# Writing the Fourier stage of the next group into the inverse's own tile, and keeping the inverse's matrices in SBUF

## The chip, the cores and the metric

One core of a Trainium2 chip runs the whole program. It has TensorE (PE, the products), VectorE (DVE), ScalarE (ACT), GpSimd (POOL) and SyncE (SP), which here only issues DMAs. The metric is the time of the device for one execution, in microseconds; runs of the kernel before lie between 3988.0 and 3996.9 us.

## The reference

Three parts in a row, all in float32. The change touches the first.

```
X = np.fft.rfft(x, axis=1)                     # x: 8 x 3072 x 256
Y = X * (filt_r + 1j * filt_i)[None]
y = np.fft.irfft(Y, n=3072, axis=1)            # then rows of 24576 tokens x 256
# routing: one of 8 experts by argmax of x @ w_gate, its gates, h = relu(x @ w1[e]) @ w2[e]
# then relu(x @ w_in)**2 @ w_out
```

## The kernel before

**Groups.** The 8 sequences go in four groups of two; the real and the imaginary part of a transform carry one sequence each. A sequence of 3072 is 64 x 48 (N1 x N2), so a transform is a first stage over 64 points with twiddles (48 products with a 128 x 128 matrix from `c_ma`), and a second stage over 48.

**Stage a** (`steps_a`, 12 steps a group, four of the 48 products each): x comes by DMA (`load_x`, 512 KB a step, two steps ahead). In group 0 the x tile is the stationary operand, so the product comes out with channels on the partitions; it is copied into `big`, an SBUF tile of 128 channels x 2 halves x 96 rows x 64 points (L269 to L274). In groups 1 to 3 the matrix is the stationary operand (L282); the product is copied into `ao` and written to rows in DRAM (`s1`, L287).

**Stage b** (`steps_b`, 32 units and a lag of three, so 35 steps a group), the middle stage. It takes two of the 64 points at a time. In group 0 `turn_b` transposes them out of `big` on PE (four transposes, L320) and copies them into `bi`, by turns on ScalarE and VectorE (L322). In groups 1 to 3 `load_b` reads `bi` from `s1` by DMA, four units ahead. Then `b_first` multiplies with the second stage's matrix (L347, L351), ScalarE copies the result crosswise into `q` (L353, L354), VectorE and GpSimd multiply with the filter (L355, L356); `b_mid` adds (L364), which frees the PSUM tile (three of them); `b_second` goes back through the inverse's first stage (L373) and ScalarE copies into `big` (L375), at the place of the two points. Each step issues the first part of one unit, the middle of the unit before and the second part of the unit three before.

**Stage c** (`steps_c`, 24 units and a lag of one, 25 steps a group), the inverse's last stage. A unit is two of the 48 rows. `c_turn` turns a row out of `big` and multiplies it with the gate weights (L394); `c_first` multiplies with the inverse's matrix (L410), a 512 KB tile for 8 rows. Those come by DMA, six a group and two buffers (`load_m(mi, ...)`, L403 and L538). After every four units `route` computes the gates and places of 8 x 128 tokens on VectorE with two small products on PE (L452, L462); the rows go to DRAM in one write of 1088 KB (L485), and 8 scatters of GpSimd (`scatter`, L423, two in each step of stage c) put the row numbers into one of four tables in DRAM by turns.

**The order.** All engines get their work in the order of one string, `order` (L526 to L547), a letter a step; each engine works through its own in that order. Group 0's 12 a steps stand first. Then, for each group, its 35 b steps and its 25 c steps; six a steps of the next group stand between the b steps (after 8, 16, 24 and the last three), six between the first c steps, and the first three b steps of the next group stand between the last three c steps. `ahead` holds loads to be issued at a place of the order. SP's queue takes the DMAs in the order of issue; a DMA that waits holds up those behind it. The experts' matrices and first products begin in the last group's stage c.

Of the kernel before, what the change touches and what calls it, by code (L numbers as in the profile page):

```python
# [23 lines left out]
E, F1 = 8, 1024  # L24
# [4 lines left out]
GC = D  # L29
PK = GC + 16  # L30
SEG = NT
# [69 lines left out]
def spectral_moe_kernel(ctx: ExitStack, tc: tile.TileContext, x, filt_r, filt_i, w_gate, w_og, w1, w2,  # L101
# [5 lines left out]
    dram = ctx.enter_context(tc.tile_pool(name="dram", bufs=1, space=DRAM))  # L107
    s1 = [dram.tile([96 * N1, PK], F32, name=f"s1_{g}") for g in range(NG)]
    yd = dram.tile([NT + 1, YW], F32, name="yd")
# [21 lines left out]
    cum_bf = const.tile([TC * E, TC * E + E], BF16, name="cum_bf")  # L131
    cum_f = const.tile([TC * E, TC * E + E], F32, name="cum_f")
    nc.scalar.dma_start(out=cum_f, in_=c_cum)
    nc.vector.tensor_copy(cum_bf, cum_f)

# [6 lines left out]
    for i in range(2):  # L142
# [21 lines left out]
    zrow = fcon.tile([1, YW], F32, name="zrow")  # L164
    nc.gpsimd.memset(zrow, 0.0)
    mb = fcon.tile([96, 2, 128], F32, name="mb")
    mb2 = fcon.tile([128, 2, 96], F32, name="mb2")
    sg = fcon.tile([128, 3], F32, name="sg")
    KF = 2
    NFB = 4  # L170
    fbuf = [fcon.tile([128, 2, KF, D], F32, name=f"fb{i}") for i in range(NFB)]
    map_, xp, aop, bip, qp = (right(fft, n, b) for n, b in (("map", 6), ("xp", 3), ("aop", 3), ("bip", 6), ("qp", 4)))
    psP = right(fft, "psP", 3, space=PSUM)
# [12 lines left out]
    mip, vtp, yop, rp, psA, psL = (inv.enter_context(tc.tile_pool(name=n, bufs=b, **kw)) for n, b, kw in (  # L186
        ("mip", 2, {}), ("vtp", 4, {}), ("yop", 4, {}), ("rp", 2, {}), ("psA", 3, {"space": PSUM}), ("psL", 1, {"space": PSUM})))
    big = ccon.tile([128, 2, 2 * N2, N1], F32, name="big")
# [65 lines left out]


    def steps_a():
        for u in range(len(aunits)):
            g, i = aunits[u]
            if g == 0 and i % 2 == 0 and i // 2 + 1 < 6:
                load_m(ma, c_ma, map_, i // 2 + 1)  # L260
            if u + 2 < len(aunits):
                load_x(u + 2)
            t = xt.pop(u)
            if g == 0:
                for h in range(JA // 2):
                    ps = psA.tile([128, 2, D], F32, name="p")
                    for j in range(2):
                        n = JA * i + 2 * h + j
                        for c in range(2):  # L269
                            at = (2 * h + j) * D + c * 128  # L270
                            nc.tensor.matmul(ps[:, c, j * 128:(j + 1) * 128], t[:, at:at + 128], ma[n // 8][:, n % 8, :])
                    n = 2 * (JA * i + 2 * h)
                    (nc.scalar.copy if h == 0 else nc.vector.tensor_copy)(
                        big[:, :, n:n + 4, :].rearrange("p c r k -> p c (r k)"), ps)  # L274
                yield
                continue
            ao = aop.tile([128, JA, D], F32, name="ao")
            for h in range(JA // 2):
                ps = psA.tile([128, 2, D], F32, name="p")
                for j in range(2):  # L280
                    n = JA * i + 2 * h + j
                    nc.tensor.matmul(ps[:, j], ma[n // 8][:, n % 8, :], t[:, (2 * h + j) * D:(2 * h + j + 1) * D])  # L282
                if h == 0:
                    nc.scalar.copy(ao[:, 0:2], ps)
                else:
                    nc.vector.tensor_copy(ao[:, 2:4], ps)
            later.append(lambda g=g, i=i, ao=ao: nc.sync.dma_start(  # L287
                out=s1[g][i * JA * 128:(i + 1) * JA * 128, 0:GC].rearrange("(j q) c -> q j c", j=JA), in_=ao))
            yield


    LAG = 3
    AB = 4
    s1v = [s.rearrange("(m k) c -> m k c", k=N1) for s in s1]
    ks = []
# [12 lines left out]

    def load_b(u):
        g, at = units[u][0], place(u)  # L310
        bi[u] = bip.tile([96, 2, D], F32, name="bi")
        nc.sync.dma_start(out=bi[u], in_=s1v[g][:, at:at + 2, 0:D])

    def turn_b(u):
# [9 lines left out]
    def b_first(u):  # L324
        g, ka, kb, w, up = units[u]
        v = u % UB
        if v + AB < UB and g:
            load_b(u + AB)
        if v == 0 or not up or v == UB - 1:
            nw = g * NW + w + 2  # L330
            for _ in fl[0]:
                pass
            if nw < NG * NW:
                fl[0] = load_f(nw)
        next(fl[0], None)
        next(fl[0], None)
        if v == UB - 1:
            for _ in fl[0]:
                pass
        if v == 0:  # L340
            dup_f(g * NW)
        if v == 0 or up and v < UB - 1:
            dup_f(g * NW + w + 1)
        f = fbuf[(g * NW + w) % NFB]
        p = psP.tile([128, 512], F32, name="p")
        if not up:
            nc.tensor.matmul(p, mb[:, up], bi.pop(u).rearrange("p k d -> p (k d)"))  # L347
        else:
            b = bi.pop(u)
            for k in range(2):  # L350
                nc.tensor.matmul(p[:, k * D:(k + 1) * D], mb[:, up], b[:, 1 - k])  # L351
        q = qp.tile([128, 512], F32, name="q")
        nc.scalar.copy(q[64:128], p[0:64])  # L353
        nc.scalar.copy(q[0:64], p[64:128])  # L354
        nc.vector.tensor_tensor(p, p, f[:, 0].rearrange("p k d -> p (k d)"), ALU.mult)  # L355
        nc.gpsimd.tensor_tensor(q, q, f[:, 1].rearrange("p k d -> p (k d)"), ALU.mult)  # L356
        pq[u] = p, q
# [42 lines left out]
    def c_first(u):  # L400
        g, j = cunits[u]
        if j % 4 == 0 and j + 4 < UC:
            load_m(mi, c_mi, mip, 6 * g + j // 4 + 1)  # L403
        c, s = divmod(u, 4)
        if s == 0:
            yo[c] = yop.tile([128, TC, YW], F32, name="yo")
        for i in range(2):
            n = 2 * j + i
            ps = (psL if i or g == NG - 1 else psO).tile([128, 512], F32, name="o")[:, 0:YW]
            nc.tensor.matmul(ps, mi[6 * g + n // 8][:, n % 8, :], vt.pop((u, i)))  # L410
            (nc.vector.tensor_copy if i else nc.scalar.copy)(yo[c][:, 2 * s + i], ps)
# [16 lines left out]
    def route(c):  # L428
# [3 lines left out]
        l = yo[c][:, :, HD:HD + 2 * E]  # L432
        m = rp.tile([128, TC, 1], F32, name="m")
        nc.vector.tensor_reduce(m[:, :, 0], l[:, :, 0:E], AX.X, ALU.max)
        d = rp.tile([128, TC, E], F32, name="d")
        nc.vector.tensor_tensor(d, l[:, :, 0:E], m.to_broadcast([128, TC, E]), ALU.subtract)
        cd = rp.tile([128, TC, E], F32, name="cd")
        nc.vector.scalar_tensor_tensor(cd, d, 0.0, rev, op0=ALU.is_ge, op1=ALU.mult)
        mx = rp.tile([128, TC, 1], F32, name="mx")
        nc.vector.tensor_reduce(mx[:, :, 0], cd, AX.X, ALU.max)  # L440
# [3 lines left out]
        nc.vector.tensor_copy(ob, oh.rearrange("p a e -> p (a e)"))  # L444
        z = rp.tile([128, TC, E], F32, name="z")
        nc.vector.tensor_tensor(z, oh, l[:, :, E:2 * E], ALU.mult)
# [20 lines left out]
        t = yo.pop(c)  # L467
        s = rp.tile([128, TC], F32, name="s")
        rk = rp.tile([128, TC, E], F32, name="rk")
        si = rp.tile([128, TC], I32, name="si", bufs=4)  # L470
        sl = rp.tile([128, TC], F32, name="sl")
        nc.vector.tensor_reduce(s, ex, AX.X, ALU.add)
# [17 lines left out]
    def steps_b():  # L490
        for g in range(NG):
            for u in range(g * UB, (g + 1) * UB + LAG):
                if u == 0:
                    turn_b(0)
                    turn_b(1)
                if u + 2 < UB:
                    turn_b(u + 2)
                if u < (g + 1) * UB:
# [26 lines left out]

    order = "a" * (UA + 0)  # L526
    ahead = {}
    for g in range(NG):
        next_a = lambda: "a" if g + 1 < NG and order.count("a") < (g + 2) * UA else ""
        nb = order.count("b") - g * (UB + LAG)  # L530
        first = len(order) - 2 if g == 0 else first_b
        if g:
            ahead.setdefault(first - (1 if g == 0 else 6), []).extend(lambda u=g * UB + i: load_b(u) for i in range(AB))
        for i in range(nb, UB + LAG):
            order += "b"
            if i in (8, 16, 24) or i >= UB:
                order += next_a()
        ahead.setdefault(len(order) - 8, []).append(lambda g=g: load_m(mi, c_mi, mip, 6 * g))  # L538
        for i in range(UC + LAGC):
            order += "c"  # L540
            if i in (1, 3, 6, 8, 11, 13):
                order += next_a()
            if i >= UC - 2 and g + 1 < NG:
                if i == UC - 2:
                    first_b = len(order)
                order += "b"
    order += "--"  # L547
# [617 lines left out]
```

## Time and profile before

| | |
|---|---|
| median of three runs | 3988.5 us (3988.0 to 3996.9) |
| profiled execution | 3993.0 us, its span 3991.3 us |
| PE busy, share of the span | 96% |
| VectorE, ScalarE, GpSimd | 70%, 50%, 20% |
| mean granted clock of PE | 0.979 |
| DMA, mean over the span | 92 GB/s |

The span is the time from the first to the last instruction in the trace. The shares are means over a transform part of some 730 us and two expert parts with other limits. A granted clock of 1.0 is 2.4 GHz, 0.5 is 1.2 GHz.

### The profile page before, as it was taken

To read this page: it belongs to the slowest core of one execution; us is meant where nothing else is said; L and a number is where in the kernel's file an instruction comes from. 1 tells how busy PE (TensorE), PEld (TensorE's weight loads), DVE (VectorE), ACT (ScalarE), POOL (GpSimd) and SP (SyncE) were. 2 spreads that over 40 slices of the span, in tenths; PEclk is the share of its full clock that TensorE was granted. 3 is DMA by queue.
4 is the path that set the end of the run, shared out by engine and by line. 5 is a ranking of instruction groups with operands and counts; after the bars stand their busy time and mean duration, and the time that the engine had idled before them with its cause. 6 is when DMAs were issued, how large, how long until landed. Compare 5 with 4: busy or idle time off the path is not lost.

```text
span 3991.3 us, 73834 instructions
## 1 busy us (share of the span) xinstructions
PE 3815.1 (96%) x26884; PEld 3538.1 (89%) x26884; DVE 2800.1 (70%) x5143; ACT 1979.2 (50%) x3909; POOL 778.6 (20%) x743
## 2 busy tenths in 40 slices
PE   8897977899999999999899999999999999999998
PEld 7775756688888888888899999999999999999998
DVE  6565665478888876666577777777777777777775
ACT  5453543245545455555455555555555555555554
POOL 3354555321111121111010100100101101001001
PEclk9988988999999999999999999999999999999999
DMA  6878864255556555555100000000000000000000
GB/s 198 206 182 185 205 147 117 53 165 164 166 163 174 168 168 161 158 164 158 56 26 27 26 29 22 28 28 22 28 28 24 26 28 26 29 22 27 28 17 17
DMA packets 311184, 365.86 MB, mean 92 GB/s; under 512 B 83329, under 2 KB 253538, under 8 KB 307746
## 3 DMA queue, kind: packets, MB, share of 16 engines
q1 hardware_dynamic: 284544, 306.91, 28.3%
q0 software_dynamic: 25248, 53.99, 4.5%
q8 instruction: 211, 3.46, 0.4%
q14 instruction: 155, 1.27, 0.1%
q10 hardware_dynamic: 1026, 0.23, 0.0%
HBM read 259.87 MB, written 101.13 MB: 90 GB/s over the span
## 4 chain that ended last, share of the span: by engine, by line
PE 81%; DMA 5%; DVE 3%; issue 2%; ACT 2%; POOL 1%; SPq 0%; another core or an unknown queue 0%; POOLq 0%; DVEq 0%; ACTq 0%
PE py L952 27%; PE ph L906 17%; PE ph L823 13%; PE py L839 13%; PE px L906 7%; DMA tab<-rowid,si 3%; PE o L410 1%; PE px L801 1%; PE p L351 1%; DVE q L364 1%; PE p L394 1%; DMA m<-c_mi_dram 1%; DVE p L355 1%; PE o L373 1%; PE p L282 0%
## 5 line engine op out<-in xcount | busy, mean ns | idle before, releaser
L952 PE MATMUL py<-woh,hh 128*128 128x256 f32 x3072 | 859.6, 280 | 0.0
L952 PE MATMUL py<-woh,hl 128*128 128x256 f32 x3072 | 857.0, 279 | 0.4 <-DVE hl L939 0.4
L952 PE MATMUL py<-wol,hh 128*128 128x256 f32 x3072 | 853.7, 278 | 0.0
L952 PEld LDWEIGHTS py<-woh,hh 128*128 128x128 f32 x3072 | 578.1, 188 | 0.0
L952 PEld LDWEIGHTS py<-wol,hh 128*128 128x128 f32 x3072 | 577.8, 188 | 0.0
L952 PEld LDWEIGHTS py<-woh,hl 128*128 128x128 f32 x3072 | 576.3, 188 | 0.9 <-DVE hl L939 0.8
L961 POOL DMA_INDIRECT out_dram<-ou,io x192 | 207.9, 1083 | 1886.5 <-ACT C L928 1651.3
L827 ACT ACTIVATE hh<-ph 128x512 fp32r<-128x512 f32 (+1 forms) x496 | 261.0, 526 | 612.4 <-PE ph L823 537.0
L906 PE MATMUL ph<-bh,wsh 128*128 128x256 f32 x1920 | 540.7, 282 | 9.8 <-ACT bh L883 5.7
L906 PE MATMUL ph<-bl,wsh 128*128 128x256 f32 x1920 | 538.6, 281 | 0.0
L906 PE MATMUL ph<-bh,wsl 128*128 128x256 f32 x1920 | 536.6, 279 | 0.0
L828 DVE SCALAR_TENSOR_TENSOR hl<-ph,hh 128x512 fp32r<-128x512 f32 (+1 forms) x496 | 296.7, 599 | 259.3 <-ACT hh L827 225.5
L930 DVE SCALAR_TENSOR_TENSOR q<-C 128x1024 f32<-128x1024 f32 x384 | 468.8, 1221 | 1.2 <-ACT C L928 1.2
L939 DVE TENSOR_TENSOR hl<-q,hh 128x1024 fp32r<-128x1024 f32 x384 | 467.0, 1216 | 1.1 <-ACT hh L937 1.1
L924 DVE TENSOR_TENSOR C<-ph,p 128x256 f32<-128x256 f32 x384 | 163.2, 425 | 412.4 <-ACT hh L937 331.9
L937 ACT CAST hh<-q 128x1024 fp32r<-128x1024 f32 x384 | 404.4, 1053 | 1.3 <-DVE q L930 1.3
L928 ACT COPY C<-ph 128x256 f32<-128x256 f32 x384 | 143.3, 373 | 503.6 <-PE ph L906 503.6
L763 POOL DMA_INDIRECT xg<-yd,idx x190 | 201.0, 1058 | 924.5 <-DVE idx L773 864.6
L906 PEld LDWEIGHTS ph<-bh,wsh 128*128 128x128 f32 x1920 | 360.6, 188 | 12.5 <-ACT bh L883 5.8
L906 PEld LDWEIGHTS ph<-bl,wsh 128*128 128x128 f32 x1920 | 362.1, 189 | 0.1
L839 PE MATMUL py<-hh,wh 128*128 128x512 f32 (+1 forms) x992 | 361.7, 365 | 0.0
L906 PEld LDWEIGHTS ph<-bh,wsl 128*128 128x128 f32 x1920 | 361.5, 188 | 0.0
(266 smaller groups left out, 8587.1 us busy)
## 6 DMA issues: line engine op xcount, KB each, us to landing
r<-in_moe_w_dram SPq DMA_DIRECT2D x472, 256.0 KB
yd<-yo SPq DMA_DIRECT2D x24, 1088.0 KB
xt<-in_x_dram SPq DMA_DIRECT2D x48, 512.0 KB
r<-ytd SPq DMA_DIRECT2D x48, 512.0 KB
ytd<-yt SPq DMA_DIRECT2D x41, 512.0 KB
s<-ao SPq DMA_DIRECT2D x36, 512.0 KB
bi<-s SPq DMA_DIRECT2D x96, 192.0 KB
m<-c_mi_dram SPq DMA_DIRECT2D x24, 512.0 KB
```

What stands on the lines that cost most here:

```text
L763: nc.gpsimd.indirect_dma_start(out=xg[:, c * YW:(c + 1) * YW], out_offset=None, in_=yd[0:(NT * GP // NG if t < KP else NT) + 1], in_offset ...
L823: nc.tensor.matmul(ps, a[:, c, f2 * 128:(f2 + 1) * 128], b[:, c, 0:w], start=n == 0, stop=n == 5)
L827: nc.scalar.activation(hh, ps, AF.Relu)
L828: nc.vector.scalar_tensor_tensor(hl, ps, 0.0, hh.bitcast(F32), op0=ALU.max, op1=ALU.subtract)
L839: nc.tensor.matmul(Y[t][h], a[:, f % 2, h * 128:(h + 1) * 128], b, start=f == 0 and i == 0, stop=f == NF - 1 and i == 2)
L906: nc.tensor.matmul(ps, x[:, u, a], y[:, b], start=start and n == 0, stop=n == 2, skip_group_check=True)
L924: nc.vector.tensor_tensor(C[:, 3], V, p5, ALU.add)
L930: nc.vector.scalar_tensor_tensor(q, C, 0.0, C, op0=ALU.max, op1=ALU.mult)
L937: nc.scalar.copy(hh, q)
L939: nc.vector.tensor_tensor(hl, q, hh.bitcast(F32), ALU.subtract)
L952: nc.tensor.matmul(Z[t][k][:, c, :], x[:, 2 * i + k, c * 128:(c + 1) * 128], w[:, 2 * u + i, :], start=u == 0 and m in (0, 6), stop=u == N ...
L961: nc.gpsimd.indirect_dma_start(out=out, out_offset=bass.IndirectOffsetOnAxis(ap=io[:, c:c + 1], axis=0), in_=ou[:, c, :], in_offset=None)
```

## The change

All four groups now have group 0's form of stages a and b: the product of stage a is copied into `big`, and stage b transposes out of it. `s1`, `ao`, `load_b` and their DMAs are gone. Since `big` still holds what stage c of the group before reads, the a steps of the next group all stand in stage c, one after every second c step: a step i writes the eight rows that c steps 2i and 2i+1 have turned. No a steps stand between b steps any more, and no b steps in stage c. Five of the 12 x tiles of the next group are loaded during stage b, the others five steps ahead (six x buffers in place of three). The inverse's six matrix tiles are loaded once, during group 0's stage b, and stay (six buffers in place of two). To make room, `bi` has four buffers in place of six, `vt` three in place of four, some scratch tiles of `route` one in place of two, and the tile `cum_f` is given back with the transform's others.

```diff
-    s1 = [dram.tile([96 * N1, PK], F32, name=f"s1_{g}") for g in range(NG)]
...
+    XB = 6
...
-    map_, xp, aop, bip, qp = (right(fft, n, b) for n, b in (("map", 6), ("xp", 3), ("aop", 3), ("bip", 6), ("qp", 4)))
+    map_, xp, bip, qp = (right(fft, n, b) for n, b in (("map", 6), ("xp", XB), ("bip", 4), ("qp", 4)))
...
-        ("mip", 2, {}), ("vtp", 4, {}), ("yop", 4, {}), ("rp", 2, {}), ("psA", 3, {"space": PSUM}), ("psL", 1, {"space": PSUM})))
+        ("mip", 6, {}), ("vtp", 3, {}), ("yop", 4, {}), ("rp", 2, {}), ("psA", 3, {"space": PSUM}), ("psL", 1, {"space": PSUM})))
...
+    XA = 2, XB - 1
+
     def steps_a():
         for u in range(len(aunits)):
             g, i = aunits[u]
             if g == 0 and i % 2 == 0 and i // 2 + 1 < 6:
                 load_m(ma, c_ma, map_, i // 2 + 1)
-            if u + 2 < len(aunits):
-                load_x(u + 2)
+            if i + XA[g > 0] < UA:
+                load_x(u + XA[g > 0])
             t = xt.pop(u)
...
-            ao = aop.tile([128, JA, D], F32, name="ao")
             for h in range(JA // 2):
                 ps = psA.tile([128, 2, D], F32, name="p")
                 for j in range(2):
                     n = JA * i + 2 * h + j
-                    nc.tensor.matmul(ps[:, j], ma[n // 8][:, n % 8, :], t[:, (2 * h + j) * D:(2 * h + j + 1) * D])
...
+                    for c in range(2):
+                        at = (2 * h + j) * D + c * 128
+                        nc.tensor.matmul(ps[:, c, j * 128:(j + 1) * 128], t[:, at:at + 128], ma[n // 8][:, n % 8, :])
+                n = 2 * (JA * i + 2 * h)
+                (nc.scalar.copy if h == 0 else nc.vector.tensor_copy)(
+                    big[:, :, n:n + 4, :].rearrange("p c r k -> p c (r k)"), ps)
             yield
...
-        if v + AB < UB and g:
-            load_b(u + AB)
...
-        if j % 4 == 0 and j + 4 < UC:
-            load_m(mi, c_mi, mip, 6 * g + j // 4 + 1)
...
-            nc.tensor.matmul(ps, mi[6 * g + n // 8][:, n % 8, :], vt.pop((u, i)))
+            nc.tensor.matmul(ps, mi[n // 8][:, n % 8, :], vt.pop((u, i)))
...
-                if u == 0:
-                    turn_b(0)
-                    turn_b(1)
-                if u + 2 < UB:
-                    turn_b(u + 2)
+                v = u - g * UB
+                for k in (0, 1, 2) if v == 0 else (v + 2,) if v + 2 < UB else ():
+                    turn_b(g * UB + k)
...
-        for i in range(nb, UB + LAG):
+        for i in range(UB + LAG):
+            if g == 0 and i >= 8 and i % 4 == 0 and i // 4 < 8:
+                ahead.setdefault(len(order), []).append(lambda i=i: load_m(mi, c_mi, mip, i // 4 - 2))
+            if g + 1 < NG and i % 5 == 3 and i // 5 < XB - 1:
+                ahead.setdefault(len(order), []).append(lambda u=(g + 1) * UA + i // 5: load_x(u))
             order += "b"
-            if i in (8, 16, 24) or i >= UB:
-                order += next_a()
-        ahead.setdefault(len(order) - 8, []).append(lambda g=g: load_m(mi, c_mi, mip, 6 * g))
         for i in range(UC + LAGC):
             order += "c"
-            if i in (1, 3, 6, 8, 11, 13):
-                order += next_a()
-            if i >= UC - 2 and g + 1 < NG:
-                if i == UC - 2:
-                    first_b = len(order)
-                order += "b"
+            if g + 1 < NG and i % 2 and i < UC:
+                order += "a"
     order += "--"
```

## Rows read from the trace of the kernel before

**Rows 1.** The page: busy us and share of the span by engine, instructions.
```profile
PE 3815.1 (96%) x26884; PEld 3538.1 (89%) x26884; DVE 2800.1 (70%) x5143; ACT 1979.2 (50%) x3909; POOL 778.6 (20%) x743
```

**Rows 2.** By stage: us, busy us by engine, granted clock, DMA share, GB/s.
```profile
0.00:38.47 38.47, 25.84 (x193) 24.52 (x193) 12.51 (x21) 8.31 (x13) 3.42 (x25) 1.00 0.88 284
38.47:120.68 82.21, 80.87 (x528) 69.78 (x529) 68.95 (x103) 64.75 (x118) 41.03 (x32) 1.00 0.48 146
120.68:195.56 74.88, 64.78 (x356) 54.55 (x355) 40.64 (x143) 26.51 (x73) 24.41 (x26) 0.93 0.87 226
195.56:283.00 87.44, 77.34 (x401) 62.63 (x400) 62.43 (x102) 54.72 (x102) 52.88 (x44) 0.86 0.69 170
283.00:362.58 79.58, 65.38 (x356) 54.69 (x355) 40.64 (x143) 26.61 (x73) 31.90 (x34) 0.94 0.93 218
362.58:454.10 91.52, 74.31 (x400) 60.24 (x399) 62.27 (x102) 54.64 (x102) 55.64 (x47) 0.87 0.67 162
454.10:531.21 77.11, 65.87 (x356) 54.82 (x355) 40.98 (x143) 26.61 (x73) 28.87 (x30) 0.96 0.98 208
531.21:619.24 88.03, 64.94 (x352) 51.64 (x351) 59.30 (x98) 51.23 (x96) 55.77 (x49) 0.83 0.50 126
```

**Rows 3.** Waits of PE, 38 to 620 us: us in total, times, longest.
```profile
PE p L347 <- DVE q L364: 36.8, 4, 17.1
PE o L410 <- DMA m<-c_mi_dram: 25.6, 6, 9.6
```

**Rows 4.** Chain that ended last, 0 to 740 us: start, us, what.
```profile
339.15 10.92 DMA tab<-rowid,si
```

**Rows 5.** Windows of the scatters (L423) alone.
```profile
284.60:374.40 89.80, 37.35 (x39) 0.90 0.88 204
616.60:631.20 14.60, 10.61 (x12) 0.93 0.11 9
```

**Rows 6.** Timeline of PE, group 0's middle stage: start, us, what, idle before it.
```profile
38.47 1.56 PE L320 MATMUL p<-ident,big 128*96 128x128 f32 x12 [0.88 <-DVE big L273]
...
45.16 1.10 PE L347 MATMUL p<-bi,mb 96*128 96x512 f32 x2 [1.14 <-DVE q L364]
...
57.79 1.92 PE L282 MATMUL p<-xt,m 128*128 128x256 f32 x8
59.55 0.60 PE L320 MATMUL p<-ident,big 128*96 128x128 f32 x4
```

**Rows 7.** Timeline of PE, group 0's last stage.
```profile
125.28 0.65 PE L394 MATMUL p<-idw,big 128*128 128x144 f32 x4
...
126.23 0.65 PE L394 MATMUL p<-idw,big 128*128 128x144 f32 x4
...
136.72 0.24 PE L452 MATMUL p<-ones_bf,ob 128*64 128x128 bf16 x1
...
138.98 0.76 PE L394 MATMUL p<-idw,big 128*128 128x144 f32 x4
```

**Rows 8.** Timeline of PE, group 0's first stage.
```profile
28.42 3.81 PE L271 MATMUL p<-m,xt 128*128 128x128 f32 x32 [0.48 <-DMA xt<-in_x_dram]
```

**Rows 9.** Timeline of GpSimd.
```profile
42.27 2.58 POOL L356 TENSOR_TENSOR q<-q,fb 128x512 f32<-128x512 f32 x2 [38.09 <-DMA tab<-zi]
...
140.90 1.18 POOL L423 DMA_INDIRECT tab<-rowid,si  x1 [26.62 <-DVE si L481]
...
733.39 0.96 POOL L423 DMA_INDIRECT tab<-rowid,si  x1 [3.33 <-DMA tab<-rowid,si]
```

**Rows 10.** DMA issues: what, queue, count, KB each.
```profile
yd<-yo SPq DMA_DIRECT2D x24, 1088.0 KB
xt<-in_x_dram SPq DMA_DIRECT2D x48, 512.0 KB
```

**Rows 11.** Timeline of SP's queue, last stage of group 3.
```profile
724.99 0.32 SPq L485 DMA_DIRECT2D yd<-yo  x1
```

More of the change, by code (lines that the diff above doesn't have):

```diff
@@ L29 @@
 GC = D
-PK = GC + 16
 SEG = NT
@@ L131, in spectral_moe_kernel @@
     cum_bf = const.tile([TC * E, TC * E + E], BF16, name="cum_bf")
-    cum_f = const.tile([TC * E, TC * E + E], F32, name="cum_f")
-    nc.scalar.dma_start(out=cum_f, in_=c_cum)
-    nc.vector.tensor_copy(cum_bf, cum_f)
     tid = const.tile([NTILE_T, 1], F32, name="tid")
@@ L165, in spectral_moe_kernel @@
     nc.gpsimd.memset(zrow, 0.0)
+    cum_f = fcon.tile([TC * E, TC * E + E], F32, name="cum_f")
+    nc.scalar.dma_start(out=cum_f, in_=c_cum)
+    nc.vector.tensor_copy(cum_bf, cum_f)
     mb = fcon.tile([96, 2, 128], F32, name="mb")
@@ L260, in steps_a @@
                 load_m(ma, c_ma, map_, i // 2 + 1)
-            if u + 2 < len(aunits):
-                load_x(u + 2)
+            if i + XA[g > 0] < UA:
+                load_x(u + XA[g > 0])
             t = xt.pop(u)
[L264 to L276, printed above, removed]
-            ao = aop.tile([128, JA, D], F32, name="ao")
             for h in range(JA // 2):
@@ L281, in steps_a @@
                     n = JA * i + 2 * h + j
-                    nc.tensor.matmul(ps[:, j], ma[n // 8][:, n % 8, :], t[:, (2 * h + j) * D:(2 * h + j + 1) * D])
[L283 to L288, printed above, removed]
+                    for c in range(2):
[4 more added lines that the diff above has]
+                    big[:, :, n:n + 4, :].rearrange("p c r k -> p c (r k)"), ps)
             yield
     LAG = 3
-    AB = 4
-    s1v = [s.rearrange("(m k) c -> m k c", k=N1) for s in s1]
     ks = []
@@ L307, in place @@
         return min(k1_place(k) for k in units[u][1:3])
[L309 to L312, printed above, removed]
     def turn_b(u):
@@ L432, in route @@
         l = yo[c][:, :, HD:HD + 2 * E]
-        m = rp.tile([128, TC, 1], F32, name="m")
+        m = rp.tile([128, TC, 1], F32, name="m", bufs=1)
         nc.vector.tensor_reduce(m[:, :, 0], l[:, :, 0:E], AX.X, ALU.max)
@@ L436, in route @@
         nc.vector.tensor_tensor(d, l[:, :, 0:E], m.to_broadcast([128, TC, E]), ALU.subtract)
-        cd = rp.tile([128, TC, E], F32, name="cd")
+        cd = rp.tile([128, TC, E], F32, name="cd", bufs=1)
         nc.vector.scalar_tensor_tensor(cd, d, 0.0, rev, op0=ALU.is_ge, op1=ALU.mult)
-        mx = rp.tile([128, TC, 1], F32, name="mx")
+        mx = rp.tile([128, TC, 1], F32, name="mx", bufs=1)
         nc.vector.tensor_reduce(mx[:, :, 0], cd, AX.X, ALU.max)
@@ L444, in route @@
         nc.vector.tensor_copy(ob, oh.rearrange("p a e -> p (a e)"))
-        z = rp.tile([128, TC, E], F32, name="z")
+        z = rp.tile([128, TC, E], F32, name="z", bufs=1)
         nc.vector.tensor_tensor(z, oh, l[:, :, E:2 * E], ALU.mult)
@@ L467, in route @@
         t = yo.pop(c)
-        s = rp.tile([128, TC], F32, name="s")
-        rk = rp.tile([128, TC, E], F32, name="rk")
+        s = rp.tile([128, TC], F32, name="s", bufs=1)
+        rk = rp.tile([128, TC, E], F32, name="rk", bufs=1)
         si = rp.tile([128, TC], I32, name="si", bufs=4)
-        sl = rp.tile([128, TC], F32, name="sl")
+        sl = rp.tile([128, TC], F32, name="sl", bufs=1)
         nc.vector.tensor_reduce(s, ex, AX.X, ALU.add)
@@ L522, in steps_c @@
                 yield
-    order = "a" * (UA + 0)
+    order = "a" * UA
     ahead = {}
     for g in range(NG):
[L529 to L533, printed above, removed]
-        for i in range(nb, UB + LAG):
+        for i in range(UB + LAG):
[3 more added lines that the diff above has]
+                ahead.setdefault(len(order), []).append(lambda u=(g + 1) * UA + i // 5: load_x(u))
             order += "b"
-            if i in (8, 16, 24) or i >= UB:
-                order += next_a()
-        ahead.setdefault(len(order) - 8, []).append(lambda g=g: load_m(mi, c_mi, mip, 6 * g))
         for i in range(UC + LAGC):
             order += "c"
-            if i in (1, 3, 6, 8, 11, 13):
-                order += next_a()
-            if i >= UC - 2 and g + 1 < NG:
-                if i == UC - 2:
-                    first_b = len(order)
-                order += "b"
+            if g + 1 < NG and i % 2 and i < UC:
+                order += "a"
     order += "--"
```

## The prediction

> **What bounds the kernel now.** The page first: TensorE (PE) is busy for 96% of the span [rows 1], which says where a saved microsecond must come from, PE's waits or PE's work. Then the busy time by stage: I cut the first 619 us where the timeline shows the last-stage and first-stage instructions begin [rows 2]. The reader is to see two kinds of stage. The middle stage of group 0 (38.47 to 120.68) has PE busy for 80.9 of 82.2 us at full clock: PE sets its time. The same stage of groups 1 to 3 has fewer PE instructions and takes longer (87.4, 91.5, 88.0 us) with PE busy for 77, 74 and 65 us and a mean granted clock of 0.83 to 0.87. The inverse's last stage of groups 0 to 2 takes 74.9, 79.6 and 77.1 us with about 65 us of PE. So this part of the kernel isn't bound by PE's work, whatever the page's 96% says. The remaining 3,370 us (the last stage of group 3 and the experts) the change hardly touches.
>
> Third, the waits of PE in that stretch [rows 3]: 36.8 us in four waits for L364, one at the start of each middle stage, and 25.6 us for the inverse's matrices by DMA (L410). Why L364 is late shows in the chain that ended last, asked for this stretch alone [rows 4]: at the end of group 1's last stage its pieces are GpSimd's scatters to the routing tables, one landing after another, as the piece of 10.9 us shown. There are four tables, so scatter n waits for the landing of scatter n-4. GpSimd's multiply (L356), which L364 needs, stands behind them in its queue. Their pace [rows 5]: 39 in 89.8 us, 2.30 us each, while the DMA engines are 88% busy at 204 GB/s, but 12 in 14.6 us, 1.22 us each, where they are 11% busy.
>
> **What the change does, part by part.** Summed against the profiled execution: 3993.0 us (span 3991.3), 4.5 us over the median of the runs.
>
> *Middle stages.* All four become group 0's without its first-stage steps. Group 0 has six of these between; one takes 1.76 us, from 57.79 to 59.55 [rows 6]. 82.21 - 6 x 1.76 = 71.65 us each. That holds the 128 transposes of a group, their copies to SBUF by VectorE and ScalarE, and the filling of the pipeline; VectorE at 69.0 and ScalarE at 64.8 of 82.2 us [rows 2] cover the copies. Were that cover gone, each of 96 steps would grow by what its copy is late.
>
> *Last stages of groups 0 to 2.* A half step (one turn, one product) is 0.95 us, 125.28 to 126.23; a route's small products cost 0.5 us (136.72 to 138.98 is 2.26, less one first-stage step of 1.76) [rows 7]. A first-stage step of the new form is 16 products of 128 columns in place of 8 of 256: two of them in 3.81 us with the tail of the last [rows 8], so 1.76 to 1.9; I take 1.8. 48 x 0.95 + 12 x 1.8 + 6 x 0.5 = 70.2 us. VectorE's 40.6 us and ScalarE's 26.6 us there [rows 2] hold the copies of six such steps and all else; twelve would have to cost 1.7 times VectorE's whole to reach 70. The writes into `big` follow reads that stand ahead of them on PE, so they add no wait.
>
> *Sum at PE's pace.* 38.47 + 4 x 71.65 + 3 x 70.2 = 535.7 us, where the last stage of group 3 began at 619.2: 83.6 us less. In it are the DMA waits of rows 3 for matrices and x, since matrices stay and x is asked for five steps ahead.
>
> *Scatters.* What the sum leaves out is GpSimd. The next group's L356 still stands behind the scatters. The first scatter of a group starts 20.2 us into its last stage (140.90) [rows 9], for the first route needs as many steps as before. By the order 34 of a group's 48 fall into its own stage (two a step from the eighth step on), 14 into the next group's. With pace r the last ends at 20.2 + 33 r + 0.96. L356 is wanted 3.8 us after the first transpose (38.47 to 42.27) [rows 6, 9], that is 74.0 us after the stage began, and without slack, since PE waits 1.14 us for L364 in group 0 already [rows 6]. The stall is 33 r - 52.8 us, where positive. In groups 1 and 2 the 14 come first; they can start when the last L356 of the stage before is done, three steps of lag of 71.65 / 32 = 2.2 us or some 6 us ahead: 47 r - 79.0, larger from r = 1.9 on. Up to r = 1.6 there is no stall.
>
> What is r? Lower bound 1.22, upper 2.30 [rows 5]. The stage's DMA falls from 226 GB/s x 74.9 us = 16.9 MB [rows 2] to six writes of 1088 KB and seven loads of 512 KB [rows 10]: 10.35 MB, 147 GB/s. Two estimates. Between the two rows in proportion to the rate: 1.22 + 1.08 x 138 / 195 = 1.98. Or from one write of routed rows alone: after one was issued at 724.99 [rows 11] four scatters go out, and the fifth waits 3.33 us, to 733.39 [rows 9]; each route brings one write and 8 scatters: (8 x 1.22 + 3.33) / 8 = 1.64. I take 1.75, nearer the second, which is this stage's own pattern (the x loads are 3.7 of its 10.35 MB): a stall of 5.0 us, 15 for three.
>
> A rule speaks against this estimate: the Trainium skill (DMA: Bandwidth & Descriptors, section Queues, rings and completion order) has each DMA engine take turns between its queues, a packet at a time. By that a scatter hardly waits for a bulk write on another queue, r stays at 1.22 and the sum has no stall, some 3904 us. The trace disagrees as far as it goes: 1.22 and 2.30 us by load [rows 5].
>
> *Clock.* Groups 1 to 3 lose 13 to 17% of the granted clock in their middle stage, 12 to 15 us each [rows 2], partly because two scatters stand between each of the first three L356. After the change none does. Between nothing and 12 us a group; I take 3, 9 in all, since one stall remains but not a row of them.
>
> *Small terms.* With six x tiles SP asks earlier in group 0's first stage, whose DMA engines are idle for 12% of 38.5 us [rows 2]: 0 to 4.6 us; 2. In the last stage of group 3 matrix waits go too; those of the other groups are 4.3 us on the mean and 9.6 at most [rows 3]: 0 to 9.6; 2. The last route of a group now runs beside a middle stage whose VectorE is 84% busy (69.0 of 82.2) [rows 2]: a wait of 0 to 2 us a group, an estimate; 3 lost. Group 0's middle stage now carries six matrix and five x loads of 512 KB where six x loads and six writes stood: nothing. Smaller buffers elsewhere (`vt`, `bi`, the routes' scratch): their users are in order on one engine or long done; nothing.
>
> 83.6 - 15 - 9 + 2 + 2 - 3 = 60.6: 3993.0 - 60.6 = 3932.4, and against the median 4.5 less, 3928 us.
>
> **The rivals.** *No stall*, r from 1.22 to 1.6: 83.6 + 1 less, 3904 us; with the small terms at their best (4.6 + 9.6 - 0) 3891. For it: 10 of 17 MB remain, and scatters without load never wait [rows 5]. Against: each write of routed rows begins where its scatters do [rows 9, 11]. 0.25.
>
> *The pace stays* at 2.30: stalls of 23.1 + 2 x 29.1 = 81.3 and 9 for the clock eat the 83.6 + 1: 3994, no change. For it: 10 of 17 MB remain. 0.05. *Slower*: the same mechanism from r = 2.35 on, where the stalls are 88 us and the time 4000; at 2.45 it is 100 us and 4013. For it: the stage's x loads now all fall into its first 14 steps, beside the writes. Against: the 2.30 was at 204 GB/s, 1.4 times the 147. 0.04.
>
> *Writes ordered against reads*: if a product of the first stage and the next turn, in the one tile `big`, are kept in order though they don't overlap, PE waits for each last copy; the first transpose of group 0 shows its price, 0.88 us [rows 6]. 36 x 0.88 = 32 us: 3960. Against: in group 0 transposes read `big` between copies into it (L375) without a wait (the one at 59.55) [rows 6]. 0.06.
>
> **How the numbers follow.** My forecast, r from 1.6 to 2.0, has 0.6: 3928 us, by itself 3905 to 3970 (r = 2.0 and 8 us of clock a group take 13.2 + 2 x 15.0 + 24 = 67: 3971). The range 3894 to 3966 takes in the first rival, the forecast up to r = 1.95 and the writes in order, and leaves out 0.15 to 0.2. A measurement tells 0.3%, 12 us, from no change. Faster 0.91 (0.6 + 0.25 + 0.06), same 0.05, slower 0.04.
>
> **What would show it.** In the profile after: middle stages of 72 us plus a stall at their start, last stages of 70 us with PE busy throughout and no wait for `c_mi`; PE's stall behind L364 at three places and nowhere else above 3 us; scatters at 1.6 to 2.0 us. The prediction is wrong if scatters hold 2.3 us, if L394 waits for L273, or if the middle stages take over 75 us without a stall.

## The result: 0.96% slower, and the profile after

The changed kernel takes 4026.76 us (median of 4, 4025.63 to 4031.47) where the kernel before takes 3988.27 in the same comparison: a ratio of 1.0096, 95% interval 1.0077 to 1.0115. The forecast was 3928 us and 0.91 for faster; the time lies above the range. Its profiled execution has a span of 4023.9 us, 32.6 more than before's 3991.3.

The page of the kernel after, busy time by engine: PE works 79 us more than in [rows 1] and has 672 instructions more.

```profile
PE 3894.2 (97%) x27556; PEld 3632.5 (90%) x27556; DVE 2834.4 (70%) x5191; ACT 2007.0 (50%) x3957; POOL 775.6 (19%) x743
```

The kernel after by stage, cut as [rows 2] are and carried on: the last stage of group 3 with the first expert product, then the second expert product alone (columns as there).

```profile
0.00:35.97 35.97, 25.20 (x193) 24.26 (x193) 12.51 (x21) 8.32 (x13) 3.43 (x25) 1.00 0.89 304
35.97:109.31 73.34, 70.81 (x480) 60.66 (x481) 65.63 (x98) 61.65 (x112) 41.04 (x32) 1.00 0.56 164
109.31:187.96 78.65, 74.15 (x495) 66.44 (x496) 40.64 (x144) 27.50 (x75) 32.34 (x34) 0.98 0.44 106
187.96:265.43 77.47, 74.02 (x484) 62.54 (x484) 69.55 (x116) 61.96 (x116) 43.66 (x36) 0.98 0.38 106
265.43:351.72 86.29, 74.19 (x495) 66.05 (x496) 40.97 (x145) 27.51 (x75) 42.23 (x44) 0.97 0.49 105
351.72:429.06 77.34, 74.16 (x484) 62.23 (x484) 69.74 (x116) 61.92 (x115) 44.83 (x37) 0.97 0.36 97
429.06:514.51 85.45, 74.91 (x496) 67.53 (x496) 41.16 (x145) 27.50 (x75) 40.31 (x42) 0.95 0.51 106
514.51:595.77 81.26, 78.01 (x484) 65.18 (x484) 69.87 (x117) 62.01 (x115) 46.72 (x39) 0.92 0.20 48
595.77:1918.32 1322.55, 1265.65 (x6670) 1077.85 (x6671) 911.45 (x1940) 614.04 (x1056) 267.27 (x266) 0.98 0.54 149
1918.32:4008.22 2089.90, 2082.85 (x17279) 2079.65 (x17280) 1512.83 (x2352) 1053.82 (x2206) 209.95 (x188) 1.00 0.08 25
```

The kernel before, the same two last stretches, which [rows 2] leave out:

```profile
619.24:1933.80 1314.56, 1261.36 (x6671) 1074.71 (x6671) 911.83 (x1940) 613.24 (x1056) 276.80 (x268) 0.98 0.54 152
1933.80:3975.61 2041.81, 2034.11 (x17279) 2030.42 (x17280) 1500.57 (x2352) 1051.74 (x2206) 204.06 (x188) 1.00 0.08 25
```

Three sums tell where the 32.6 us are. Group 3's last stage begins at 595.77, not 619.24: 23.5 us gained (forecast: 58.5). From there to the second expert product 8.0 us are lost, 1322.55 less 1314.56. The second expert product loses 48.1: same 17,280 products, same full clock, PE with gaps of 7 to 8 us in all in either, 2089.90 us for 2041.81. That stage isn't in the diff. Each product in it simply takes 2.8 ns more. Groups by line in a stretch of 500 us inside it, of the kernel after and then of the kernel before (mean ns after the busy time):

```profile
L917 PE MATMUL py<-woh,hh 128*128 128x256 f32 x741 | 209.7, 283 | 0.0
L917 PEld LDWEIGHTS py<-woh,hh 128*128 128x128 f32 x741 | 142.3, 192 | 0.0
```

```profile
L952 PE MATMUL py<-woh,hh 128*128 128x256 f32 x760 | 212.7, 280 | 0.0
L952 PEld LDWEIGHTS py<-woh,hh 128*128 128x128 f32 x759 | 142.8, 188 | 0.0
```

In the transform the middle stages of groups 1 to 3 take 77.5, 77.3 and 81.3 us, near the forecast's 80.7 (71.65 and 5.0, 3 and 1 for stall, clock and route), though without a long stall. But the last stages of groups 0 to 2 last 78.7, 86.3 and 85.5 us, not 70.2. Waits of all engines, 100 to 720 us, kernel after; "remote" is an end that the profile can't put down to any queue of this core:

```profile
ACT vt L374 <- remote: 17.6, 5, 4.2
DVE big L273 <- remote: 10.7, 2, 5.4
ACT yo L386 <- remote: 7.1, 5, 2.4
```

The timeline of all engines there (start, us, what) shows what is odd (`...` marks lines left out): PE's 16 products of a first-stage step run from 268.41 to 270.36, yet VectorE's copy of their result and SP's load into the x tile that they free start together at 272.95, 2.6 us later. (The profile names L371 as what released the copy; that product only ended last before it, and stands behind it in the program's order.)

```profile
268.41 1.95 PE L271 MATMUL p<-m,xt 128*128 128x128 f32 x16
...
272.09 0.65 PE L371 MATMUL p<-idw,big 128*128 128x144 f32 x4
272.25 0.96 POOL L398 DMA_INDIRECT tab<-rowid,si  x1 [0.30 <-issue]
272.95 0.35 SPq L207 DMA_DIRECT2D xt<-in_x_dram  x1
272.96 0.69 DVE L273 COPY big<-p 128x512 f32<-128x512 f32 x1 [3.91 <-PE p L371]
```

### The profile page after: what moved, and what is told of

The parts are those of the page before. It is cut to its first block, busy times and chain, and to the rows that moved or that the text cites. A ratio compares the mean times of both kernels' runs of the same rounds, so it can differ in the third digit from the quotient of the medians.

```text
span 4023.9 us, 74984 instructions
## 1 busy us (share of the span) xinstructions
PE 3894.2 (97%) x27556; PEld 3632.5 (90%) x27556; DVE 2834.4 (70%) x5191; ACT 2007.0 (50%) x3957; POOL 775.6 (19%) x743
## 3 DMA queue, kind: packets, MB, share of 16 engines
q1 hardware_dynamic: 242976, 259.71, 23.5%
## 4 chain that ended last, share of the span: by engine, by line
PE 91%; DVE 3%; DMA 3%; issue 1%; ACT 1%; another core or an unknown queue 0%; SPq 0%; POOL 0%; ACTq 0%; POOLq 0%; DVEq 0%
PE py L917 27%; PE ph L871 17%; PE ph L788 13%; PE py L804 12%; PE px L871 7%; PE o L350 3%; PE p L371 2%; PE o L385 2%; PE p L271 2%; PE p L324 1%; PE p L299 1%; PE p L328 1%; PE px L766 1%; DMA raw<-in_moe_w_in_dram 1%; DVE hl L793 0%
## 5 line engine op out<-in xcount | busy, mean ns | idle before, releaser
L917 PE MATMUL py<-woh,hl 128*128 128x256 f32 x3072 | 869.6, 283 | 0.4 <-DVE hl L904 0.4
L917 PE MATMUL py<-wol,hh 128*128 128x256 f32 x3072 | 869.5, 283 | 0.0
L917 PE MATMUL py<-woh,hh 128*128 128x256 f32 x3072 | 869.5, 283 | 0.0
L917 PEld LDWEIGHTS py<-woh,hl 128*128 128x128 f32 x3072 | 589.9, 192 | 0.6 <-DVE hl L904 0.6
L917 PEld LDWEIGHTS py<-wol,hh 128*128 128x128 f32 x3072 | 589.9, 192 | 0.0
L917 PEld LDWEIGHTS py<-woh,hh 128*128 128x128 f32 x3072 | 589.9, 192 | 0.0
L871 PE MATMUL ph<-bh,wsl 128*128 128x256 f32 x1920 | 544.9, 284 | 0.0
L871 PEld LDWEIGHTS ph<-bh,wsh 128*128 128x128 f32 x1920 | 370.2, 193 | 10.9 <-ACT bh L848 5.2
L871 PEld LDWEIGHTS ph<-bl,wsh 128*128 128x128 f32 x1920 | 370.3, 193 | 0.2 <-DVE bl L849 0.2
L871 PEld LDWEIGHTS ph<-bh,wsl 128*128 128x128 f32 x1920 | 370.3, 193 | 0.0
```

The lines of the kernel that those rows point to most:

```text
L871: nc.tensor.matmul(ps, x[:, u, a], y[:, b], start=start and n == 0, stop=n == 2, skip_group_check=True)
L917: nc.tensor.matmul(Z[t][k][:, c, :], x[:, 2 * i + k, c * 128:(c + 1) * 128], w[:, 2 * u + i, :], start=u == 0 and m in (0, 6), stop=u == N ...
```

## The experiments

Theory A, placement, formed from the address list of the two programs. `cum_f` (288 bytes a partition) left the pool `const`, so every later tile on the left side of SBUF starts 288 bytes lower, the expert weights of the second product among them (`wsh`, `woh`); the operands that they meet in PE (`bh`, `hh2`), on the right side, stayed. Here "distance" is that between the two operands of a product, weights and activations, whichever of them is the stationary one. Rival B is that the new order slows the experts in another way.

```
              wsh     woh     bh      hh2     distance of the two operands (bh less wsh, hh2 less woh), modulo 256
before        21504   78848   200672  149472  224, that is 32 off a multiple of 256
after         21216   78560   200672  149472  0
```

After the first comparison, that of the result, the kernels ran in three more, each on one chip with its own runs of the kernel before; so ratios are compared, and times only within a comparison.

| run | comparison | median us | before us | ratio (95%) |
|---|---|---|---|---|
| e1_before_cum_moved | 2 | 4016.6 | 3973.6 | 1.0111 (1.0094 to 1.0127) |
| e2_after_left32 | 2 | 3933.9 | 3973.6 | 0.9892 (0.9873 to 0.9911) |
| e3_after_right32 | 2 | 3939.2 | 3973.6 | 0.9912 (0.9895 to 0.9928) |
| e4_after_both32 | 2 | 3922.6 | 3973.6 | 0.9871 (0.9854 to 0.9889) |
| e5_after_again | 3 | 4026.8 | 3997.1 | 1.0080 (1.0060 to 1.0099) |
| e6_after_128 | 3 | 4014.7 | 3997.1 | 1.0041 (1.0024 to 1.0058) |
| e7_after_64 | 3 | 3966.1 | 3997.1 | 0.9934 (0.9913 to 0.9954) |
| e8_left32_mult_dve | 3 | 3966.2 | 3997.1 | 0.9927 (0.9905 to 0.9949) |
| e9_before_64 | 4 | 3964.9 | 3973.8 | 0.9975 (0.9964 to 0.9987) |
| e10_after_best64 | 4 | 3927.9 | 3973.8 | 0.9888 (0.9872 to 0.9905) |
| e11_best64_mult_dve | 4 | 3903.0 | 3973.8 | 0.9829 (0.9813 to 0.9845) |
| e12_best64_spread | 4 | 3891.5 | 3973.8 | 0.9801 (0.9784 to 0.9819) |

### Placement: e1 to e4

e1, the kernel before (here and below, `...` marks code left out):

```diff
-    cum_f = const.tile([TC * E, TC * E + E], F32, name="cum_f")
...
+    cum_f = fcon.tile([TC * E, TC * E + E], F32, name="cum_f")
```

> The kernel before with one part of the change alone: the constant cum_f (288 bytes a partition) is moved from the pool `const` to `fcon`. Every later tile on the left side of SBUF then starts 288 bytes lower, the resident expert weights wsh at byte 21216 instead of 21504. Order, queues, DMAs and the work are those of before. Theory A (placement): the second expert product's matmuls go from one each 116 to 118 ns to one each 120.0 ns as in the changed kernel, and the time rises by the 47 us which that stage lost (2047.9 to 2095.1 us): 4035 us. Rival B (the change's new order, or where its stages leave the queues, slows the experts): no change, 3988 us within 6.

e2, the changed kernel:

```diff
+    pad_l = const.tile([128, 8], F32, name="pad_l")
+    nc.gpsimd.memset(pad_l, 0.0)
```

> The changed kernel with a 32-byte tile added to `const`, so that everything after it on the left side starts 32 bytes higher: wsh at 21248, which is a multiple of 64 as 21504 was and 21216 is not. Theory A with multiples of 64 bytes as what counts: the second expert product returns to 116 to 118 ns and the time falls by 47 us to 3980 us, under the kernel before. Theory A with another grid (21504 is a multiple of 512, 21248 is not): 4027 us. Rival B (the new order): 4027 us within 6.

e3, the changed kernel (e4 has both tiles):

```diff
+    pad_r = right(ctx, "padr", 1).tile([128, 8], F32, name="pad_r")
+    nc.gpsimd.memset(pad_r, 0.0)
     fcon = right(fft, "fcon", 1)
```

> The changed kernel with a 32-byte tile at the top of the right side, so that all right-side tiles start 32 bytes lower (xh, wh, hh of the first expert product, bh and hh2 of the second: all at multiples of 64, where they were 32 off), while the left side stays 32 off. Theory A with multiples of 64: in the second product one operand of two is now in place, as in the kernel before, so it goes at 116 to 118 ns (47 us less); in the first product both are, and its 128x512 products, 227 ns apart, come towards 213 ns (512 columns at 2.4 per ns): up to 54 us less for some 3970 of them, 26 us for the 256-column ones: 3900 to 3980 us. Rival B: 4027 us within 6.

> Both 32-byte tiles at once: all operands of both expert products start at multiples of 64. Theory A: the second product's spacing falls from 120.0 ns to its 106.7 ns of columns (256 at 2.4 per ns), at most 17280 x 13.3 ns = 230 us, and the first one's as in the run with the right side alone, at most 80 us: 3717 us at the lowest, and in any case below both single moves. If only the resident weights' place counts, 3980 us. Rival B: 4027 us within 6.

The second product's stage in e1, e2, e3 and e4, one window each:

```profile
1909.76:3998.89 2089.13, 2081.97 (x17280) 2078.27 (x17280) 1512.02 (x2352) 1051.92 (x2206) 209.95 (x188) 1.00 0.08 25
```
```profile
1876.36:3916.69 2040.33, 2032.60 (x17279) 2028.78 (x17280) 1500.11 (x2352) 1051.51 (x2206) 204.69 (x188) 1.00 0.08 25
```
```profile
1876.02:3916.04 2040.02, 2032.43 (x17280) 2028.62 (x17280) 1500.00 (x2352) 1051.13 (x2206) 204.95 (x188) 1.00 0.08 25
```
```profile
1874.04:3901.54 2027.50, 2019.29 (x17279) 2015.10 (x17280) 1500.43 (x2352) 1049.52 (x2206) 204.06 (x188) 1.00 0.08 25
```

e1 is the loss without the change: the stage takes 2089.1 us and the kernel is 1.1% slower. e2 is the change without the loss: 32 bytes bring the stage back to 2040.3 us and make the changed kernel 1.1% faster than before. So the loss is placement, and rival B is out as its cause. Two expectations failed. The first product was to gain in e3, since its operands moved onto multiples of 64; its stretch with group 3's last stage takes 1292.7 us in e3 and 1290.5 in e2. And in e4, with all operands on multiples of 64, the second product was to fall far below one product in 117 ns; it gained 0.7 ns more (2040.3 less 2027.5 is 12.8 us, over 17,280). Not each operand's own place, then, but the distance of the two fits: e3 moves both operands of the first product by the same 32 bytes. e2 at 3934, not 3980, was the other surprise: the chip of this comparison is faster for the kernel before too (3973.6), and none of its four profiles holds a wait on "remote".

### Distance: e5 to e7

```diff
+    pad_l = const.tile([128, 32], F32, name="pad_l")        # e7: 16
...
-        for stack, name, bufs, kw in ((xgs, "xgp", 2, {}), (xgs, "hp", 4, {}), (m1, "wrp", 3, {}), (m1, "whp", 4, {}),
+        for stack, name, bufs, kw in ((xgs, "xgp", 2, {}), (xgs, "hp", 4, {}), (m1, "padp", 1, {}), (m1, "wrp", 3, {}), (m1, "whp", 4, {}),
...
+            if name == "padp":
+                nc.gpsimd.memset(pl[name].tile([128, 32], F32, name="pad_m"), 0.0)        # e7: 16
```

> The changed kernel once more, unchanged, beside the kernel before on one chip, because the two profiles of the first comparison hold waits of ScalarE and VectorE that end on no event the profile names (17.6 us for vt alone in the changed kernel), and none of the four runs since holds one. If these waits belong to the changed kernel, its last stages of groups 0 to 2 are again 80 to 89 us long and it is again 38 us slower than before. If they belong to the moment, the stages are 72 us as in the run with the left side moved by 32 bytes, and of the 38 us there remains what placement costs less what the stages gain: about 49 - 34 = 15 us.

> The changed kernel with a 128-byte tile in `const` (all later left-side tiles 128 bytes higher: wsh at 21344) and a 128-byte tile between hp and wrp (the first product's weights wh 128 bytes lower: 141984). No operand changes its place within 64 bytes: all stay 32 off. Only the distance between the weights and the moving operand changes, by 128 bytes, modulo 256 from 0 to 128, in both products of both stages. Theory A1 (each operand's own place on a 64-byte grid counts): no change, 120.0 ns in the second product and 119.4 and 227 ns in the first, 4027 us. Theory A2 (the distance of the two operands counts; it was a multiple of 256 in the changed kernel, 32 off one in the kernel before and in both single moves, 64 off in the run with both): the second product goes at 116.5 ns or less, 60 us less or more, and the first product's too falls by about as many ns each, 5952 x 3 = 18 us: 3950 us or less.

> As the run before with 64 bytes in place of 128: distance 64 off a multiple of 256, all operands still 32 off a multiple of 64. Theory A1: no change, 4027 us. Theory A2: the second product as in the run with both sides moved, 116.1 and 117.0 ns (62 us less), the first product's below 119.4 ns: 3960 us or less. By comparison with 128 it also shows whether the gain grows with the distance.

The two last stretches of e5, e6 and e7:

```profile
593.89:1918.85 1324.96, 1262.08 (x6670) 1075.17 (x6670) 912.00 (x1940) 613.66 (x1056) 272.61 (x266) 0.98 0.54 149
1918.85:4007.39 2088.54, 2081.48 (x17279) 2078.17 (x17280) 1513.11 (x2352) 1051.83 (x2206) 207.27 (x188) 1.00 0.08 25
```
```profile
596.58:1932.63 1336.05, 1277.77 (x6671) 1074.74 (x6671) 911.34 (x1940) 614.11 (x1056) 280.54 (x267) 0.98 0.54 148
1932.63:3999.20 2066.57, 2059.31 (x17280) 2055.49 (x17280) 1501.94 (x2352) 1053.98 (x2206) 205.21 (x188) 1.00 0.08 25
```
```profile
596.96:1912.88 1315.92, 1261.46 (x6671) 1069.19 (x6671) 910.67 (x1940) 613.02 (x1056) 277.12 (x267) 0.99 0.55 150
1912.88:3942.65 2029.77, 2022.11 (x17279) 2018.23 (x17280) 1502.62 (x2352) 1048.47 (x2206) 203.84 (x188) 1.00 0.08 25
```

With every operand still 32 off a multiple of 64, e7's second product takes 2029.8 us, as in e4, whose distance is the same 64: theory A1, each operand's own place on a grid of 64 bytes, is out, and A2, the distance, stands. But the gain doesn't grow with the distance: at 128 it is 22 us, at 64 it is 59, and e6 at 4015 us missed the 3950 or less expected of it; e7 came to 3966 where 3960 or less was expected. In the first product, whose two operands were a multiple of 256 apart before the change too, 64 gave 9 us here and 128 cost 11; e10 against e4 (1293.0 and 1292.0) finds nothing for 64 there, so that gain isn't established.

That 256 is the period can be read from the same addresses. Modulo 512 the distances of the kernel before and of e2 are 480 and 224, and the stage takes 2041.8 and 2040.3 us; in e9 and e10 below they are 448 and 192, and it takes 2029.1 and 2031.9. So 256 bytes more change little. 128 do change it: 2088.5 in e5, 2066.6 in e6. Every run moved a whole side or all tiles behind a pad, so the distance of the weights to other tiles of the right side moved along.

e5 repeats the first comparison, on a chip where the kernel before takes 3997 us: +0.8%, with waits on "remote" and last stages of 78.0, 85.1 and 76.4 us again. By itself that is what was expected if the waits were the changed kernel's. But all four profiles of this comparison hold such waits, and so does before's of the first; none of the eight in the two others does. They belong to the chip or the moment, not to the change. What they are stays open.

### The change's own worth, and the scatters: e8 to e12

e8 (on e2) and e11 (on e10):

```diff
-        nc.gpsimd.tensor_tensor(q, q, f[:, 1].rearrange("p k d -> p (k d)"), ALU.mult)
+        (nc.vector if g and v < 8 else nc.gpsimd).tensor_tensor(q, q, f[:, 1].rearrange("p k d -> p (k d)"), ALU.mult)
```

> The kernel with the left side moved by 32 bytes, and in groups 1 to 3 the first eight multiplies by the filter's second plane of a middle stage on VectorE in place of GpSimd, whose queue then holds the last scatters of the stage before alone. Theory (what is left of the stall is GpSimd's queue, 38.0 us of PE waits for the combine in that run): the three middle stages fall from 79.8, 91.5 and 88.3 us to 72 to 77, with up to 8 x 0.70 us of VectorE's time each as the price: 20 to 35 us less than 3934 us. Rival (the stall is that of the transfers, and another wait takes its place): within 8 us of 3934.

e9 is the kernel before, e10 the changed one, both with tiles as above that set all distances to 64.

> The kernel before, with no part of the change, with 32 bytes added in `const` (wsh at 21536) and a 64-byte tile between hp and wrp, so that weights and moving operand are 64 off a multiple of 256 in both stages. Theory A2 (distance): the second product goes from 117.0 and 118.0 ns to 116.1 and 117.2, 12 to 14 us less; the first product's 256-column ones from 119.4 to 116.2 ns, its 512-column ones about 1 ns the other way, 0 to 8 us less: 0.3 to 0.6% under the kernel before. If the distance was not the cause, no change.

> The changed kernel with both 32-byte tiles and the 64-byte tile between hp and wrp: the same distances as the run of the kernel before with 64. Between these two the change's own worth stands alone. Theory (the stages of the transform gain 20 to 35 us as their rows say, and the experts' loss is placement and nothing else): 20 to 35 us less than that run, its second product at the same spacing within 0.2 ns. Rival (the change costs the experts in another way too): less than 15 us between them.

> The run before, with the first eight multiplies by the filter's second plane in the middle stages of groups 1 to 3 on VectorE. Where the profile of the run before has long waits of PE for the combine at the start of these stages (38.0 us in the run with the left side moved), they go, at up to 17 us of VectorE's time: 10 to 30 us less. Where the last stages are stretched by the late events, there is little to take away, and the time is the same within 8 us.

e12, on e10:

```diff
-                scatter(2)
+                scatter(2 if g == NG - 1 or u % 2 else 1)
...
                     b_first(u)
+                    if v % 2:
+                        scatter(1)
...
-        si = rp.tile([128, TC], I32, name="si", bufs=4)
+        si = rp.tile([128, TC], I32, name="si", bufs=6)
```

> The run with all three tiles, with the scatters spread: one and two in turn in each step of a last stage but group 3's, and one in every second step of a middle stage behind that step's multiply, with six buffers for their index in place of four. GpSimd then holds at most a few scatters when a middle stage begins, and the landing of one is covered by two steps (4.3 us). Theory: the waits for the combine at the start of the three stages fall to under 3 us each, 15 to 35 us less than the run without; rival: each scatter in a middle stage delays that stage's multiplies by its own 0.96 us and its wait, and the stages grow again: no change within 8 us.

e8 says little: on that chip the last stages were stretched (79.2, 79.4, 83.4 us), which leaves little queue of scatters to step around, its middle stages are 79.4, 78.6 and 78.4 us, and no run of e2 stands beside it. The other comparison is clear. e9, at 0.25% under the kernel before, falls just short of the 0.3 to 0.6 expected. e9 and e10, same distances, same chip, have 37 us between them. The last two stretches of e9 and then of e10:

```profile
631.27:1916.52 1285.25, 1252.86 (x6670) 1062.48 (x6671) 910.80 (x1940) 613.95 (x1056) 283.98 (x269) 0.99 0.56 155
1916.52:3945.64 2029.12, 2019.60 (x17280) 2015.59 (x17280) 1500.81 (x2352) 1049.32 (x2206) 204.44 (x188) 1.00 0.08 25
```
```profile
586.34:1879.29 1292.95, 1255.35 (x6670) 1065.86 (x6670) 910.97 (x1940) 613.69 (x1056) 279.41 (x267) 0.99 0.57 153
1879.29:3911.18 2031.89, 2023.96 (x17280) 2019.78 (x17280) 1503.62 (x2352) 1051.85 (x2206) 205.06 (x188) 1.00 0.08 25
```

So the change is worth 37 us at equal placement, a little over the 20 to 35 expected, and the second product lost by placement (2.8 us between the two, 0.16 ns a product). Stages of e10, the last ones of groups 0 to 2, each with the next group's middle one:

```profile
111.14:181.97 70.83, 70.83 (x495) 64.57 (x496) 40.64 (x144) 28.14 (x75) 27.61 (x29) 1.00 0.52 118
181.97:265.38 83.41, 74.62 (x485) 62.69 (x484) 71.46 (x116) 61.94 (x116) 47.86 (x41) 0.96 0.40 98
265.38:336.21 70.83, 70.83 (x495) 64.58 (x496) 41.23 (x144) 28.14 (x75) 35.44 (x38) 1.00 0.60 118
336.21:427.52 91.31, 74.90 (x484) 62.98 (x483) 70.98 (x116) 62.02 (x116) 51.64 (x44) 0.91 0.35 90
427.52:498.36 70.84, 70.83 (x496) 64.59 (x496) 41.07 (x144) 28.14 (x75) 34.67 (x37) 1.00 0.58 123
498.36:586.34 87.98, 74.53 (x484) 62.60 (x484) 71.50 (x117) 61.91 (x116) 52.01 (x45) 0.92 0.22 49
```

PE's largest wait in e10, 100 to 590 us (us in total, times, longest), and then the scatters alone in two stretches of the same run (GpSimd's busy time and their number, granted clock, DMA share, GB/s):

```profile
PE p L328 <- DVE q L345: 32.7, 4, 14.8
```
```profile
268.20:352.80 84.60, 40.86 (x43) 0.96 0.59 116
432.00:510.00 78.00, 38.26 (x40) 0.98 0.60 119
```

The last stages are PE's alone, 70.83 of 70.83 us, and the middle ones carry the forecast's stall, 32.7 us of it. In e11 the middle stages fall to 78.8, 82.1 and 79.3 us and the time by 25; in e12 to 75.9, 78.1 and 77.8 and the time by 36, to 0.978 to 0.982 of the kernel before. The same wait in e11, 100 to 565 us, and in e12, 100 to 556 us:

```profile
PE p L328 <- DVE q L345: 6.0, 5, 1.3
```
```profile
PE p L328 <- DVE q L345: 5.4, 6, 1.6
```

e11 takes multiplies out of GpSimd's queue and leaves the scatters, e12 spreads the scatters; either removes the wait. So the stall was GpSimd's queue, as the forecast had it.

## Why the prediction was wrong

The step that failed is the sentence that left the rest of the kernel out of the sum: "The remaining 3,370 us (the last stage of group 3 and the experts) the change hardly touches." The move of `cum_f` was given no cost and no rival. It moved the expert weights by 288 bytes, to a distance of a multiple of 256 from what they meet in PE, and cost 48.1 us in the second product. Without it (e2) the changed kernel stands at 0.989 of before, against the forecast's 3928 / 3988.5 = 0.985. None of the rivals was the cause.

That step isn't the whole miss of the first comparison: 4026.8 less 48.1 is 3978.7, still 12.7 above the range. The rest is the stall, for which r was too small, and the waits on "remote". Where those waits are absent and the second product is at the distance that it had before, e2 and e3 lie at 0.989 and 0.991 of the kernel before, inside the forecast's 0.976 to 0.994 (3894 and 3966 over 3988.5).

The other steps, by the runs without the unexplained waits:

- Group 0's first stage, 2 us less of at most 4.6: 2.5 in the first comparison (35.97 in place of 38.47), 5.0 between e1 and e2 (41.25 and 36.29), 4.7 between e9 and e10 (42.50 and 37.82). Sized low.
- Middle stages at 71.65 us: group 0's, which has no stall, takes 73.3. Taking six steps out saved (82.21 - 73.34) / 6 = 1.48 us each and not 1.76: PE's busy time fell by 10.06 us, 1.68 a step, and its gaps grew from 1.34 to 2.53 us. That is 6.8 us in four stages.
- Last stages at 70.2 us with PE busy throughout: 70.83. Right, and the rival of writes in `big` ordered against reads is out: e10's last stages have no gap.
- Scatters at 1.75 us and 15 us of stall: the mechanism was right, r was mis-sized. Measured are 84.60 / 43 = 1.97 and 78.00 / 40 = 1.95 us, at 116 and 119 GB/s, below the 147 that the estimate assumed; by the prediction's own formulas, 33 r - 52.8 and 47 r - 79.0, r = 1.96 is 38 us for the three groups, and the waits are 32.7 us in all, 17.7 more than forecast. The proportional estimate that I set aside, 1.98, came nearest, but in part by luck: with the measured 118 GB/s in place of 147 the same line gives 1.82. So the load alone, as a mean, doesn't set r. The Trainium skill's rule (DMA: Bandwidth & Descriptors, section Queues, rings and completion order) has engines take turns between queues, a packet at a time. The prediction drew from it a rival in which r stays at 1.22, and these rows don't agree with that.
- Clock, 9 us: the three middle stages of e10 are 42.7 us over 3 x 73.32, and 32.7 of it are the waits; 10 remain for the clock and for the last route's wait, of which the forecast had 9 and 3. Right in sum; the rows don't part the two.
- Group 3's last stage was to begin at 560.7 us (535.7 + 15 + 9 + 3 - 2). It does at 586.3 in e10, 595.8 in the first comparison, and 553.8 in e12. Of e10's 25.6 us the stall is 17.7 and the middle stages 6.8.

In the first comparison the unexplained waits turned the stall into something else: last stages of 78.7 to 86.3 us gave the scatters time, so the middle stages after them lost little to L341 (5.4 us of PE's waits in six; in e5 14.1, of which 8.4 stand behind its shortest last stage, 76.4), and the gain there was 23.5 us where e9 and e10 have 631.3 less 586.3, 45, and e1 and e2 have 620.4 less 585.9, 34.5. Between there and the second product the changed kernel is 8.0 us longer, and 7.7 in e10 than in e9, but only 1.1 in e2 (1290.5) than in e1 (1289.4). No run was made for this; whether the experts' first part gives back some of the earlier start stays open.

## What to carry to other kernels

A tile that is moved, added or removed shifts everything allocated after it: list the addresses of the hot matrix products' operands before and after, and give the shift a line in the sum, even for stages that the diff doesn't name. If a stage slows at full clock with no gap in PE, compare the mean of one instruction first; a pad of 32 bytes decided the matter here in one run. And where a queue holds work for two stages, try to spread the less urgent part over both, as e12 did, before estimating how long its tail is.

## What the runs showed of the hardware

Products of 128x256 in the second expert stage, back to back at full clock, by the distance of the two operands modulo 256 bytes: 2088.5 to 2089.9 us for the stage at 0 (three runs: 120.9 ns each, gaps included), 2040.0 to 2041.8 at 32 short of a multiple, 2027.5 to 2031.9 at 64 short, 2066.6 at 128. Distances of 32 and 64 above a multiple weren't run in this stage. So it isn't monotonic, and why the distance counts no run shows. The loads of the stationary operand go with it: 192 ns at 0, 188 at 32 short.

Waits that end on no event of the core, in the transform's stages up to 8.5 us each, came in all six profiles of two comparisons and in none of the eight of the other two. In the runs with them, the three last stages of groups 0 to 2 of the changed kernel take 250.4 us in the first comparison and 239.5 in e5, against 212.5 without; those of the kernel before take 231.6 with them, and 219.3 (e1) and 232.1 (e9) without, so a loss there isn't established. The stretch from group 3's last stage to the second product takes 1314.6 to 1325.0 us with them, in either kernel (1336.1 in e6, whose distance there is 128), and 1285.3 to 1293.0 without. That the waits cause these longer stages is argued from their coming together; no run could add or remove them.
